# One V set copied into another tile, and two stores queued behind the wait for Wo

## The chip, the cores and the metric

The kernel runs on one core of one Trainium2 chip. The metric is the device time of one execution in microseconds (us), median of several runs.

## The reference

Two layers follow each other on 2048 rows of 512 numbers. The first is an attention over segments with a memory that is handed from segment to segment, the second a gated MLP with a mixing over rows:

```python
for s in range(n_seg):                      # 64 segments of 32 rows
    h = concat([mem, xs])                   # 8 memory rows + 32 rows
    q, k, v = h @ Wq, h @ Wk, h @ Wv        # 32 heads of 128
    p = softmax(where(mask, q @ k.T * scale, -1e9))
    o = (p @ v) @ Wo
    mem = o[:, :M]                          # next segment's memory
    outs.append(o[:, M:])
h  = x + concat(outs)                       # x was normalized for the attention
z  = gelu(layernorm(h) @ w_in); z1, z2 = halves(z); z2 = layernorm(z2)
h2 = h + (z1 * (w_sp @ z2 + b_sp)) @ w_out
```

Segments depend on each other through `mem`, so the kernel runs 64 steps one after the other.

## The kernel before

**Steps and groups.** One step is one segment (`for s in range(NSEG)`). A step multiplies 32 columns: 8 memory rows and the first 24 rows of its segment. The last 8 rows of each segment are taken out of the step, 16 segments at a time: a *batched group* `ck` (four of them) holds 16 × 8 = 128 rows, whose Q, K and V are computed with full tiles, in pieces that are put between the work of earlier steps. V of a group is made as eight *sets* `n` of 128 × 512 numbers by `vx_mm(ck, n, bank)`. `vx_evac(ck, n, bank, eng)` copies a set from PSUM into an SBUF tile (ScalarE at L488, VectorE at L490) and stores it to the DRAM buffer `vext_d` (L494). Step `s` gets its part back by `load_vx(s)` into `Vx` (L511).

**The tiles.** Sets of group 0 lie in `part` (eight rows of tiles, free at the start). Sets of all later groups share the two halves of `Vs`, by turns: `vcnt` counts them in program order. `partx` holds the *batched output rows* (the output of the rows that were taken out of the steps); it is first written in step 6 and stored at L773.

**The order on the queues.** The program is written as one list; each operation goes to its engine's queue in that order, and an emitter derives its waits from names of what it reads and writes ("tokens"): who writes a tile waits for all who still read it, stores included. Nearly all DMAs are issued by SyncE (SP in the profile), in program order, so a wait ahead of one DMA holds all those behind it. An argument `after` adds a wait; `behind()` names TensorE's last instruction in the program so far.

**The start.** The weights are loaded first: Wq, Wv, Wk, and then `Wo` in four quarters (L922). Of group 0, the first two segments' piece of each set is stored at once; the pieces for segments 2 to 5 of sets 2 to 7 are put aside in `vrest[0]` and issued later, the rest (`vrest[1]`) in steps 0 to 2. In step 0 the program then has, among others: the Q, K and V of segment 0 (`QK`, L539; `V_half`, L645), the batched Q/K/V left over, set 0 of group 1 (`start_v(0, 1)`, copied by VectorE), scores (L590) and softmax, set 1 of group 1 (copied by ScalarE), and behind it these four:

```python
vx_evac(1, 1, 5, "act")
for f in vrest[0]:
    f([em.last_w[("Wo", 3)]])     # after the last quarter of Wo
wT_read(0, 0)                     # L851: a transposed read of w_sp into wst
load_xe(3, 1)                     # L303: rows of group 3 into xn
```

then `load_x(2, 0)` (L295: rows 256 to 383 into `xn`), the products with V (L670, L676), `wT_write(0, 0)` (L856), set 2 of group 1 (VectorE), the output product with `Wo` (L708, in two halves, evacuated by ScalarE at L727), the memory for the next segment (L735, L738), the first Q and K products of step 1, set 0 of group 2 (ScalarE), and the copy of the mask into PSUM for step 1 (L574). Step 1 goes on with its Q and K products, which ScalarE evacuates (`QK_evac`, L550) and VectorE transposes (L558).

Of the kernel before, what the change touches and what calls it, by code (L numbers as in the profile page):

```python
# [169 lines left out]
def fast_path(nc, st, keep, flags, A_x, A_mem0, A_Wq, A_Wk, A_Wv, A_Wo, A_seg_len, B_w_in, B_w_sp, B_b_sp, B_w_out, out):  # L170
# [25 lines left out]
    em = Emitter(n_dma_sems=40)  # L196

    def sb(name, shape, dt):
        return st.enter_context(nc.sbuf_tensor("f_" + name, shape, dt))
# [32 lines left out]
    partx = sb("partx", [128, 512], BF)  # L232
# [38 lines left out]
    def PB(b):  # L271
        return ("ps", b)

    def sp(fn, **k):
        return em.add("sp", fn, dma=True, **k)
# [4 lines left out]
    def act(fn, **k):  # L280
        return em.add("act", fn, **k)

    def dve(fn, **k):
        return em.add("dve", fn, **k)
# [13 lines left out]
    def xbuf(j):  # L298
        return (xn[:, j, :], [("xn", j)]) if j < 2 else (part[:, j, :], [("part", j, 0), ("part", j, 1)])

    def load_xe(ck, j, queue="sp"):
        t, tok = xbuf(j)
        em.add(queue, lambda e: e.dma_start(t, xe[CK * ck:CK * ck + CK, XM:SEG, :]), dma=True, writes=tok)  # L303
# [176 lines left out]
    def vx_evac(ck, n, bank, eng="act", queue="sp"):  # L480
        if ck == 0:
            t, tok = part[:, n, :], [("part", n, 0), ("part", n, 1)]
        else:
            j = vcnt[0] % 2
            vcnt[0] += 1
            t, tok = Vs[:, j, :], [("Vs", j)]
        if eng == "act":
            act(lambda e: e.activation(out=t, in_=ps[:, bank, :], func=ACT.Copy, scale=VSC), reads=[PB(bank)], writes=tok)  # L488
        else:
            dve(lambda e: e.tensor_scalar(out=t, in0=ps[:, bank, :], scalar1=VSC, scalar2=None, op0=ALU.mult), reads=[PB(bank)], writes=tok)  # L490
        def store(i0, i1, ks, queue="sp", after=()):
            r = slice(8 * i0, 8 * i1)
            dst = vext_d[ck, n, r, :, :].rearrange("p r e -> p (r e)")
            em.add(queue, lambda e: e.dma_start(dst, t[r, :]), dma=True, reads=tok, writes=[("vext", ck, n, k) for k in ks], after=after)  # L494

        if ck:
            store(0, CK, (0,), queue)
        else:
            store(0, 2, (0,), queue)
            if n < 2:  # L500
                store(2, CK, (1, 2))
            else:
                vrest[0].append(lambda after=(): store(2, 6, (1,), after=after))
                vrest[1].append(lambda: store(6, CK, (2,)))

    vcnt, vrest = [0], ([], [])
# [247 lines left out]
    def behind():  # L754
        return [em.by_eng["pe"][-1]]
# [19 lines left out]
    def px_load(rb):  # L775
        i0 = 4 * rb % 8
        for g in range(4):
            sp(lambda e, g=g: e.dma_start(part[32 * g:32 * g + M, i0:i0 + 4, :], px_d[rb, g].rearrange("j r d -> r j d")),
               reads=[("pxd", rb)] + [("part", i0 + j, k) for j in range(4) for k in range(2)], writes=[("pm", rb % 2, g)])
# [69 lines left out]
    def wT_read(i, k):  # L849
        r = slice(8 * k, 8 * k + 8)  # L850
        sp(lambda e: e.dma_start_transpose(out=wst[:, r, :], in_=B_w_sp[i * 64:(i + 1) * 64, 1024 * k:1024 * k + 1024]),  # L851
           writes=[("wst", k)], after=behind())
# [39 lines left out]
    def start_v(n, ck=0):  # L892
        start_group(vx_mm, vx_evac, ck, n)
# [27 lines left out]
    for hq in range(4):  # L921
        sp(lambda e, hq=hq: e.dma_start(w_o[:, 8 * hq:8 * hq + 8, :], wor[:, 8 * hq:8 * hq + 8, :]), writes=[("Wo", hq)])  # L922
        em.mark_const(("Wo", hq))


    class Gap:
# [23 lines left out]
    def vx_group(ck, n):  # L950
        gx.append([lambda dc=dc: vx_mm(ck, n, XB, dc) for dc in range(DC)] + [lambda: vx_evac(ck, n, XB, "dve")])

    def vx_atoms(ck, n):
        mms = [lambda ck=ck, n=n, dc=dc: vx_mm(ck, n, VXB, dc) for dc in range(DC)]
        gv.add(VXB, mms, lambda eng: vx_evac(ck, n, VXB, eng))
# [59 lines left out]
    for s in range(NSEG):  # L1015
# [3 lines left out]
            w2_load()  # L1019
        if j4 == 3 and rb > 0:  # L1020
            px_load(rb - 1)
        if s > 0:
            wT_read(s // 2, s % 2)

        def qk_piece(pi):
            QK(s, QKP[pi], range(2 if pi < 2 else 1 if pi == 2 and s else 0, DC))
# [67 lines left out]
        sm_rcp(1)  # L1094
        if s == 0:
            vx_evac(1, 1, 5, "act")
            for f in vrest[0]:
                f([em.last_w[("Wo", 3)]])
            wT_read(0, 0)
            load_xe(3, 1)  # L1100
        if s > 0:
            v_second()
        if j4 == 1:
# [965 lines left out]
def build_kernel(nc, A_x, A_mem0, A_Wq, A_Wk, A_Wv, A_Wo, A_seg_len, B_x, B_w_in, B_w_sp, B_b_sp, B_w_out, out):  # L2069
    args = (A_x, A_mem0, A_Wq, A_Wk, A_Wv, A_Wo, A_seg_len, B_w_in, B_w_sp, B_b_sp, B_w_out, out)  # L2070
    flags = {}
    with contextlib.ExitStack() as keep:
        with contextlib.ExitStack() as st:
            em, sems, dsems = fast_path(nc, st, keep, flags, *args)
# [83 lines left out]
```

## Time and profile before

| | |
|---|---|
| median of 3 runs | 838.24 us (837.37 to 839.92) |
| profiled execution | 840.62 us |
| its span, first to last instruction | 838.9 us |
| mean granted TensorE clock | 0.997 |
| TensorE busy | 824.4 us (98%) |
| VectorE / ScalarE / GpSimd busy | 475.9 / 514.2 / 145.0 us |
| DMA | 80.54 MB, mean 96 GB/s |

The profile shows one execution. PE is TensorE, PEld its weight load, DVE VectorE, ACT ScalarE, POOL GpSimd, and SP or SPq SyncE, which issues DMAs. A row of a timeline has the start in us from the span's start, the duration, engine, line, operation, output and input tile, shapes and count; in brackets stands the idle time of the engine ahead of it and who ended it. A row of the chain has start, duration and what the end of the program was waiting for at that time. A row of the windows has the stretch, its length, the busy time of each engine with its number of instructions, the granted TensorE clock (1.00 is full), the busy share of the DMA engines and GB/s. A row of the waits has the engine and line that waited, for whom, the sum in us, how many times, and the longest.

### The profile page before, as it was taken

Reading aid. Unit: us, or ns where it says so; the run is one execution under the profiler, and the core shown is the slowest. Engines: PE = TensorE matmul, PEld = TensorE weight load, DVE = VectorE, ACT = ScalarE, POOL = GpSimd, SP = SyncE. Lnnn points to the kernel's source line nnn. Section 1 sums busy time; section 2 is a strip of 40 time slices with the busy share of each in tenths; the row PEclk is TensorE's granted clock in tenths of the full one; section 3 lists DMA queues with packets and bytes.
Section 4 is the critical chain, followed back from the end, with each engine's and each line's share of the span. In section 5 each row is a group of like instructions: output and inputs, shape, how many; then the busy total and the mean of one; then the engine's idle time right before and its main releaser. Section 6 shows DMA issues by size and latency. Waiting matters only on the chain.

```text
span 838.9 us, 48365 instructions
## 1 busy us (share of the span) xinstructions
PE 824.4 (98%) x21963; PEld 484.4 (58%) x21963; DVE 475.9 (57%) x1221; ACT 514.2 (61%) x1549; POOL 145.0 (17%) x412
## 2 busy tenths in 40 slices
PE   7999999999999999999999999999999999999998
PEld 7755565656566555655566656555665554444443
DVE  3546565656566555666556556565655576653344
ACT  2467777777777777777777777676666676300000
POOL 5202111121121111112211121111111123200000
PEclk9999999999999999999999999999999999999999
DMA  9975222122222222222212122333343278223101
GB/s 313 386 214 108 69 60 68 49 68 60 61 63 58 65 60 65 63 73 58 67 50 72 48 70 72 103 85 85 78 83 84 73 253 260 90 101 103 42 13 48
DMA packets 107652, 80.54 MB, mean 96 GB/s; under 512 B 49672, under 2 KB 97040, under 8 KB 107440
## 3 DMA queue, kind: packets, MB, share of 16 engines
q1 hardware_dynamic: 105712, 74.82, 30.8%
q8 instruction: 174, 2.85, 1.5%
q10 hardware_dynamic: 1504, 2.36, 0.9%
q14 instruction: 38, 0.31, 0.1%
q0 software_dynamic: 224, 0.20, 0.1%
HBM read 43.72 MB, written 23.13 MB: 80 GB/s over the span
## 4 chain that ended last, share of the span: by engine, by line
PE 92%; SPq 5%; DMA 1%; issue 0%; ACT 0%; DVE 0%; POOL 0%; POOLq 0%
PE f_ps L539 27%; PE f_ps L708 14%; PE f_ps L645 13%; PE f_ps L1266 12%; PE f_ps L426 4%; PE f_ps L764 4%; SPq L313 3%; PE f_ps L1360 3%; PE f_ps L1259 3%; PE f_ps L670 3%; PE f_ps L476 2%; PE f_ps L830 2%; PE f_ps L590 1%; DMA f_arena<-in_A_Wo_dram 1%; SPq L922 1%; PE f_ps L1226 1%
## 5 line engine op out<-in xcount | busy, mean ns | idle before, releaser
L539 PE MATMUL f_ps<-f_arena,f_hT 128*32 128x512 bf16 (+1 forms) x5120 | 238.5, 337 | 0.4
L539 PEld LDWEIGHTS f_ps<-f_arena,f_hT 128*32 128x32 bf16 x5120 | 124.4, 96 | 89.0 <-ACT f_hT L738 20.0
L550 ACT ACTIVATE f_Tst<-f_ps 128x512 bf16<-128x512 f32 (+2 forms) x320 | 143.4, 510 | 36.1 <-PE f_ps L539 28.5
L645 PE MATMUL f_ps<-f_arena,f_hT 128*32 128x512 bf16 x2048 | 139.8, 379 | 0.0
L708 PE MATMUL f_ps<-f_arena,f_cT 128*32 128x256 bf16 x4096 | 130.1, 273 | 2.2 <-DMA f_arena<-in_A_Wo_dram 1.3
L635 POOL TENSOR_TENSOR f_E_sb<-f_R_sb,f_E_sb 128x64 bf16<-128x64 f32 x128 | 47.5, 371 | 411.0 <-ACT f_R_sb L627 411.0
L708 PEld LDWEIGHTS f_ps<-f_arena,f_cT 128*32 128x32 bf16 x4096 | 97.0, 96 | 27.5 <-ACT f_cT L694 17.3
L558 DVE STREAM_TRANSPOSE f_QT<-f_Tst 128x256 uint32<-128x256 uint32 x128 | 57.1, 446 | 93.2 <-ACT f_Tst L550 93.2
L657 DVE TENSOR_SCALAR f_V_sb<-f_ps 128x512 bf16<-128x512 f32 (+1 forms) x128 | 71.4, 558 | 52.4 <-PE f_ps L645 52.4
L1266 PE MATMUL f_ps<-f_arena 128*128 128x512 bf16 x448 | 100.5, 379 | 0.0
L1266 PEld LDWEIGHTS f_ps<-f_arena 128*128 128x128 bf16 x448 | 43.7, 98 | 52.9 <-issue 0.3
L694 ACT ACTIVATE f_cT<-f_ps 128x160 bf16<-128x160 f32 (+1 forms) x192 | 55.6, 329 | 26.0 <-PE f_ps L676 25.4
L696 DVE TENSOR_SCALAR f_cT<-f_ps 128x256 bf16<-128x256 f32 x128 | 48.4, 420 | 36.7 <-PE f_ps L676 36.7
L604 ACT ACTIVATE f_E_sb<-f_ps 128x224 bf16<-128x224 f32 x128 | 46.3, 362 | 36.6 <-PE f_ps L616 35.4
L727 ACT ACTIVATE f_part<-f_ps 128x256 bf16<-128x256 f32 x128 | 49.3, 385 | 20.6 <-PE f_ps L708 16.1
L558 DVE STREAM_TRANSPOSE f_KT<-f_Tst 128x256 uint32<-128x256 uint32 (+2 forms) x192 | 58.4, 330 | 4.5 <-ACT f_Tst L550 1.8
L645 PEld LDWEIGHTS f_ps<-f_arena,f_hT 128*32 128x32 bf16 x2048 | 47.1, 95 | 19.8 <-issue 0.4
L738 ACT ACTIVATE f_hT<-f_ps 128x16 bf16<-128x16 f32 x126 | 23.3, 185 | 45.8 <-PE f_ps L735 45.8
L1272 DVE TENSOR_TENSOR f_arena<-f_ps,f_arena 128x512 f32<-128x512 f32 x28 | 19.3, 690 | 52.5 <-PE f_ps L1266 50.5
L627 ACT ACTIVATE f_R_sb<-f_R_sb 128x160 f32<-128x160 f32 x128 | 43.3, 338 | 4.0
L576 DVE CAST f_ps<-f_mask 128x224 f32<-128x224 bf16 x80 | 29.9, 373 | 26.9 <-ACT f_hT L406 24.5
L426 PE MATMUL f_ps<-f_arena,f_hTe 128*32 128x512 bf16 x640 | 41.9, 379 | 0.0
(127 smaller groups left out, 1157.8 us busy)
## 6 DMA issues: line engine op xcount, KB each, us to landing
wT_d<-f_wst SPq DMA_DIRECT2D x64, 128.0 KB
f_arena<-wT_d SPq DMA_DIRECT2D x32, 256.0 KB
f_arena<-in_A_Wv_dram SPq DMA_DIRECT2D x4, 1024.0 KB
f_arena<-in_A_Wk_dram SPq DMA_DIRECT2D x4, 1024.0 KB
f_arena<-in_A_Wo_dram SPq DMA_DIRECT2D x4, 1024.0 KB
f_Vx<-vext_d SPq DMA_DIRECT2D x62, 64.0 KB
vext_d<-f_Vs SPq DMA_DIRECT2D x24, 128.0 KB
zp_d<-f_Vs SPq DMA_DIRECT2D x20, 112.0 KB
```

The source lines that it names most:

```text
L426: pe(lambda e, c=c, rhs=rhs: e.matmul(ps[32 * c:32 * c + 32, bank, :], lhsT=hTe[:, ck, dc, 32 * sg:32 * sg + 32], rhs=rhs, start=(dc == 0) ...
L539: pe(lambda e, dc=dc, c=c, rhs=rhs: e.matmul(ps[32 * c:32 * c + 32, bank, 0:32 * nh], lhsT=hT[:, sl, dc, :], rhs=rhs, start=(dc == 0), sto ...
L550: act(lambda e: e.activation(out=st_.rearrange("p (hp i r) -> p hp i r", i=32, r=2), in_=ps[:, bank, 0:64 * np_].rearrange("p (hp r i) -> ...
L558: dve(lambda e: e.transpose(out=dst, in_=src), reads=tok, writes=[(nm, b, k) for k in halves(b, p0, np_)])
L635: pool(lambda e: e.tensor_tensor(out=ev, in0=rv, in1=ev, op=ALU.mult), reads=[("R", b), ("Ex", b)], writes=[("Ex", b)])
L645: pe(lambda e, dc=dc, c=c, c0=c0: e.matmul(ps[32 * c:32 * c + 32, bank, 0:w], lhsT=hT[:, sl, dc, :], rhs=w_v[:, dc, c0:c0 + w], start=(dc ...
L657: dve(lambda e: e.tensor_scalar(out=dst, in0=src, scalar1=VSC, scalar2=None, op0=ALU.mult), reads=[PB(bank)], writes=tok)
L694: act(lambda e: e.activation(out=dst, in_=src, func=ACT.Copy, scale=UNSC), reads=[PB(bank)], writes=tok)
L696: dve(lambda e: e.tensor_scalar(out=dst, in0=src, scalar1=UNSC, scalar2=None, op0=ALU.mult), reads=[PB(bank)], writes=tok)
L708: pe(lambda e, h=h, g=g, i=i, b=b, c=c: e.matmul(ps[32 * g:32 * g + 32, bank, 0:d1 - d0], lhsT=cTh[:, i, 8:40], rhs=w_o[:, h, d0:d1], star ...
L727: act(lambda e: e.activation(out=part[:, s % 8, d0:d1], in_=ps[:, bank, 0:d1 - d0], func=ACT.Copy), reads=[PB(bank)], writes=[("part", s % ...
L1266: pe(lambda e: e.matmul(ps[:, bank, 0:TB], lhsT=z2[:, sc, fb * 128:(fb + 1) * 128], rhs=wTb[tb % 2][:, :, sc, :], start=first, stop=last), ...
```

## The change

Three things are edited. Set 0 of group 1 is copied into `partx` and stored from there, and does not count in the turns of `Vs`. The held pieces `vrest[0]`, with their wait for the last quarter of `Wo`, come right behind the loads of `Wo` in the program. The first transposed read `wT_read(0, 0)` and `load_xe(3, 1)` come at the top of step 0. On SyncE's queue the stores of sets 0 and 1 of group 1 now stand behind all of these.

```diff
     def vx_evac(ck, n, bank, eng="act", queue="sp"):
         if ck == 0:
             t, tok = part[:, n, :], [("part", n, 0), ("part", n, 1)]
+        elif (ck, n) == (1, 0):
+            t, tok = partx[:], ["partx"]
         else:
             j = vcnt[0] % 2
             vcnt[0] += 1
...
         em.mark_const(("Wo", hq))
+    for f in vrest[0]:
+        f([em.last_w[("Wo", 3)]])
...
-        if s > 0:
-            wT_read(s // 2, s % 2)
+        wT_read(s // 2, s % 2)
+        if s == 0:
+            load_xe(3, 1)
...
         if s == 0:
             vx_evac(1, 1, 5, "act")
-            for f in vrest[0]:
-                f([em.last_w[("Wo", 3)]])
-            wT_read(0, 0)
-            load_xe(3, 1)
```

## The prediction

> **What bounds the kernel now.** I read the page's first part, then its chain, then the chain in order of time around the four `Wo` loads, because that is the place in the program that the change touches.
>
> ```profile
> span 838.9 us, 48365 instructions
> PE 824.4 (98%) x21963; PEld 484.4 (58%) x21963; DVE 475.9 (57%) x1221; ACT 514.2 (61%) x1549; POOL 145.0 (17%) x412
> PE 92%; SPq 5%; DMA 1%; issue 0%; ACT 0%; DVE 0%; POOL 0%; POOLq 0%
> ...
> 42.84 12.13 DMA f_arena<-in_A_Wo_dram
> 54.97 0.04 issue
> 55.01 1.38 PE f_ps L708 x44
> ...
> 57.40 3.05 PE f_ps L539 x72
> 60.45 0.10 PE f_ps L590 x15
> ```
>
> TensorE is busy 98% of the span and holds 92% of the chain. So there is no slack later on in which a delay could be taken back: a microsecond in which TensorE stands still in the first steps is a microsecond at the end. The chain passes from DMA to TensorE at 54.97, when the last quarter of `Wo` lands; from 55.01 it is TensorE's, and 60.45 is the first score product of step 1.
>
> Next the place itself: SyncE's queue, and TensorE's wait.
>
> ```profile
> 50.15 2.17 SPq L494 DMA_DIRECT2D vext_d<-f_Vs  x2
> 54.99 3.31 SPq L494 DMA_DIRECT2D vext_d<-f_part  x6
> 58.34 1.33 SPq L851 DMA_TRANSPOSE f_wst<-in_B_w_sp_dram  x1
> 59.71 0.57 SPq L303 DMA_DIRECT2D f_xn<-in_A_x_dram  x1
> 60.33 0.58 SPq L295 DMA_DIRECT2D f_xn<-in_A_x_dram  x1
> 61.34 0.34 SPq L856 DMA_DIRECT2D wT_d<-f_wst  x1
> ...
> 53.17 0.55 PE L708 MATMUL f_ps<-f_arena,f_cT 128*32 128x256 bf16 x12
> 55.01 1.38 PE L708 MATMUL f_ps<-f_arena,f_cT 128*32 128x256 bf16 x44 [1.29 <-DMA f_arena<-in_A_Wo_dram]
> 57.25 3.20 PE L539 MATMUL f_ps<-f_arena,f_hT 128*32 128x512 bf16 x72
> 60.28 0.27 PE L590 MATMUL f_ps<-f_QT,f_KT 128*32 128x40 bf16 x16
> ```
>
> The two stores of 128 KB (sets 0 and 1 of group 1) are issued from 50.15. The six held rests of group 0 go out at 54.99, at once when `Wo` has landed; behind them SyncE issues without a break the transposed read (58.34), the row load L303 (59.71) and the row load L295 (60.33). TensorE's output product L708 starts with 12 matmuls, which need the first three quarters of `Wo`, and stands still 1.29 us for the fourth. That 1.29 us is all that an earlier landing of `Wo` can give.
>
> **The change part by part.** *The two large stores leave the time before 54.97.* Do they delay `Wo` now? VectorE tells, since its third copy (set 2 of group 1) writes the buffer that the first store reads:
>
> ```profile
> 55.36 0.69 DVE L490 TENSOR_SCALAR f_Vs<-f_ps 128x512 bf16<-128x512 f32 x1 [1.59 <-DMA vext_d<-f_Vs]
> 59.67 0.45 DVE L558 STREAM_TRANSPOSE f_KT<-f_Tst 128x256 uint32<-128x256 uint32 x1
> 48.00:52.00 4.00, 3.72 (x97) 1.99 (x95) 1.45 (x4) 2.95 (x8) 0.81 (x2) 1.00 1.03 330
> 52.00:55.00 3.00, 1.72 (x64) 0.90 (x64) 0.89 (x3) 1.08 (x5) 0.64 (x2) 1.00 0.40 138
> ```
>
> The store issued at 50.15 releases VectorE at 55.36, 5.2 us later and just after the last of `Wo` (54.97): what was issued later on SyncE's queue came out later, so the stores stood behind `Wo`, not before it. From 52 to 55 the engines are busy only 0.40, so `Wo`'s tail is not short of bandwidth either. Ends for the gain: 0, and 0.8 us if the 262 KB had to go through first at the 330 GB/s of the row before. I take 0, since the order of landing is the nearer evidence. [...]
>
> VectorE's 1.59 us wait goes too (set 2 now has a buffer that nobody reads yet). It gives nothing: VectorE's next work, the transposes of step 1, ends what TensorE waits for at 59.67 + 0.45 = 60.12.
>
> *The buffers change places.* Set 0 goes to the row tile, so the alternation of the two-deep `Vs` starts one set later. Before: set 0 in half 0, set 1 in half 1, set 2 in half 0, and set 0 of group 2 in half 1. After: set 1 in half 0, set 2 in half 1, and set 0 of group 2 in half 0. That last copy is ScalarE's, at the end of step 0, and now overwrites what the store of set 1 reads. It must wait until that store has landed.
>
> ```profile
> 57.49 0.18 ACT L738 ACTIVATE f_hT<-f_ps 128x16 bf16<-128x16 f32 x1 [0.37 <-PE f_ps L735]
> 57.57 0.59 ACT L488 ACTIVATE f_Vs<-f_ps 128x512 bf16<-128x512 f32 x1
> 58.05 0.37 ACT L574 ACTIVATE f_ps<-f_mask 128x224 f32<-128x224 bf16 x1
> 58.55 2.32 ACT L550 ACTIVATE f_Tst<-f_ps 128x512 bf16<-128x512 f32 x5
> ```
>
> The copy (L488) runs at 57.57 and no wait stands before it: the store of set 1 went out around 52. After the change that store stands on SyncE's queue behind the wait for `Wo` (54.99), the six rests, the transposed read and L303. Nothing of these is faster than before, so it reaches the place where L295 stands now: set 0's store at 60.33, set 1's about 0.38 us later (the 0.34 us of the equal store L856 and a gap), at 60.7. When does it land? Nearest is the same form of transfer, the 128 KB store of the row tile, with the load that waits for it:
>
> ```profile
> 115.79 0.32 SPq L773 DMA_DIRECT2D px_d<-f_partx  x1
> 118.88 1.31 SPq L778 DMA_DIRECT2D f_part<-px_d  x4
> ...
> SPq L778 <- DMA px_d<-f_partx: 23.1, 12, 2.8
> ```
>
> Twelve such waits take 23.1 us, 1.9 us each behind the issue, and this one row bounds issue to landing by 3.1 us. So 60.7 + 0.34 + 1.9 = 63.0 us. Lower end: the queue gave things out in order, and the transposed read of 58.34 had landed only when L856 was issued at 61.34; so not before 61.3. Upper end: 5.2 us as behind `Wo`, 65.9. ScalarE's copy therefore moves from 57.57 to 63.0, by 5.4 us (ends 3.7 and 8.3).
>
> Behind it on ScalarE, in program order, stand the mask copy (L574) and the five evacuations of step 1's Q and K products (L550). TensorE can still run the 72 matmuls L539 to 60.45, since their banks are free; then the score product (60.28 now) waits for transposes that wait for L550. Its slack is 60.28 − 60.12 = 0.16 us. So TensorE stops for 5.4 − 0.16, **5.2 us** (ends 3.5 and 8.1), from 60.45 to about 65.6. Nothing hides this: VectorE and GpSimd have no other work for step 1, and TensorE takes its matmuls in program order.
>
> *The clock.* The same trace shows what a standstill of this length did near the start:
>
> ```profile
> 10.65 1.57 PE L449 MATMUL f_ps<-f_hTe,f_arena 128*128 128x128 bf16 x16 [3.31 <-DMA f_arena<-in_A_Wq_dram]
> 8.00:11.00 3.00, 0.35 (x7) 0.38 (x8) 0.00 (x0) 0.00 (x0) 2.03 (x12) 1.00 1.05 378
> 11.00:14.00 3.00, 3.00 (x32) 3.00 (x30) 0.89 (x2) 0.60 (x1) 2.16 (x10) 0.50 1.05 400
> 14.00:17.00 3.00, 3.00 (x53) 3.00 (x51) 0.89 (x2) 1.62 (x4) 2.23 (x9) 0.93 1.07 364
> ```
>
> After 3.31 us of idleness the granted clock was 0.50 from 11 to 14, and 0.93 on the mean of the next 3 us, so 3 + 3 × 0.07 / 0.5 = 3.4 us at half speed. Work bound by TensorE loses half of that, 1.7 us. Ends 0 and 1.7; I take **1.0**, as ScalarE paces part of the score stage (its 2.32 us of L550 come first) and the slow stretch may begin inside the idle time. By the row alone the clock falls, as the new standstill is longer than 3.31 us. [...]
>
> *What else is moved, at nothing.* The rests of group 0, the transposed read and L303 keep their time: they were released by `Wo` before and are now; the transposed read's new condition, the first Q product of step 0, is long past. GpSimd's two early loads of `Vx` read other pieces and wait for none of this. L295 is passed by two stores and goes out 0.8 us later (61.1); its reader is VectorE's normalization in step 1, itself 5 us later. L856 and the next stores move by under 1 us behind TensorE work that moves by five. The row tile's first other use is step 6. Without that cover each would cost at most the 0.8 us of two issues.
>
> *Sum.* Against the profiled execution: 840.62 us (its span 838.9 and 1.7 outside) + 5.2 + 1.0 = 846.8. That execution lies 2.4 us above the median of the runs shown, so on the median 838.24 + 6.2 = **844.4 us**.
>
> **The rivals.** *Clock stays up*: the standstill without the slow stretch, 838.24 + 5.2 = 843.4. [...] Against it: the 0.50 after the shorter wait.
>
> *Not slower: the stores did delay `Wo`, and nothing new waits.* This needs the store of set 1 to land before ScalarE comes to the copy, that is `Wo` to land some 5 us earlier, or the copy to find another buffer. The gain would then be 0.8 us, at most the 1.29 us of TensorE's wait: 837.0 to 837.4. For it: the wait at 55.01 is real and on the chain. Against it: the order of landing, and 1.29 us is far from 5.
>
> *It does nothing*: ScalarE's copy does not meet the store, 838.2. It would need the sets to be copied in another order than the rows show (49.4, 51.4, 55.36, 57.57 by start).
>
> ```profile
> 49.43 0.69 DVE L490 TENSOR_SCALAR f_Vs<-f_ps 128x512 bf16<-128x512 f32 x1 [1.33 <-PE f_ps L476]
> 51.37 0.58 ACT L488 ACTIVATE f_Vs<-f_ps 128x512 bf16<-128x512 f32 x1
> ```
>
> **How the numbers follow.** Standstill with the slow stretch, 844.4: 0.55. Standstill alone, 843.4: 0.37. Gain without a new wait: 0.05. Nothing: 0.01. A gain from something that no row shows: 0.02. A measurement of this kernel can tell about 0.3%, 2.5 us, from no change; the small gain and the nothing lie within that, so faster 0.02, same 0.06, slower 0.92. The range goes from the shortest standstill without slow clock, 838.24 + 3.5 = 841.7, taken as 841.8, to the longest with the whole slow stretch, 838.24 + 8.1 + 1.7 = 848.0.
>
> **What would show it.** Right: ScalarE's L488 near 63 with about 5 us of idleness before it, put down to the store from `Vs`; L574, L550 and the score product shifted alike; a hole in TensorE from about 60.5 to 65.6; a second stretch at 0.50 after it; L708's 1.29 us wait for `Wo` unchanged; later steps as long as before. Wrong: L488 at its old place; or `Wo` landing well before 54.97; or the hole filled by later steps becoming shorter.

## The result, and the profile after

The changed kernel takes 844.65 us (median of 6 runs, 843.25 to 848.13) against 837.75 us (6 runs) of the kernel before: a ratio of 1.0084, with a 95% interval of 1.0062 to 1.0105. It is slower by 6.9 us. The profiled execution of the changed kernel took 844.35 us, close to its median; that of the kernel before (840.62) lay 2.9 us above its own, so the two spans differ by only 3.7 us, and the loss has to be read at its place, not from the spans.

The page's first lines and the chain in order of time (start, duration, what the end was waiting for), after:

```profile
span 842.6 us, 48367 instructions
PE 825.7 (98%) x21963; PEld 486.3 (58%) x21963; DVE 475.8 (56%) x1221; ACT 513.6 (61%) x1549; POOL 145.0 (17%) x412
```

```profile
40.52 12.29 DMA f_arena<-in_A_Wo_dram
52.81 0.04 issue
52.86 1.39 PE f_ps L710 x44
...
55.25 2.21 PE f_ps L541 x40
57.45 0.18 SPq L853
57.63 0.05 issue
57.68 0.57 SPq L303
58.25 0.05 issue
58.30 0.58 SPq L496
58.88 0.04 issue
58.92 2.12 DMA vext_d<-f_Vs
61.05 0.02 issue
61.07 0.60 ACT f_Vs L490
61.67 0.25 ACT f_ps L576
61.92 1.01 ACT f_Tst L552 x2
```

The lines of the kernel that are named here stand two lower in the file than before (L708 is now L710), save L303 and L295. Where the chain of before stayed with TensorE from 55.01 on, it now leaves it for SyncE's queue (the transposed read, the row load L303, the store of set 0), then for the store of set 1 until 61.05, ScalarE's copy, the mask, and the first two evacuations. `Wo` landed at 52.81 here and at 54.97 in the trace of before. Most of that difference is older than anything that the change touches: the first Q and K products of step 0 already start at 32.19 here and at 34.69 before. So times are counted from `Wo`'s landing.

ScalarE's timeline, then TensorE's, after:

```profile
61.07 0.60 ACT L490 ACTIVATE f_Vs<-f_ps 128x512 bf16<-128x512 f32 x1 [5.55 <-DMA vext_d<-f_Vs]
61.57 0.35 ACT L576 ACTIVATE f_ps<-f_mask 128x224 f32<-128x224 bf16 x1
61.85 2.31 ACT L552 ACTIVATE f_Tst<-f_ps 128x512 bf16<-128x512 f32 x5
```

```profile
52.86 1.39 PE L710 MATMUL f_ps<-f_arena,f_cT 128*32 128x256 bf16 x44 [1.34 <-DMA f_arena<-in_A_Wo_dram]
55.09 3.20 PE L541 MATMUL f_ps<-f_arena,f_hT 128*32 128x512 bf16 x72
63.45 0.32 PE L592 MATMUL f_ps<-f_QT,f_KT 128*32 128x40 bf16 x16 [5.16 <-DVE f_KT L560]
72.75 3.20 PE L541 MATMUL f_ps<-f_arena,f_hT 128*32 128x512 bf16 x72
```

ScalarE's copy waited 5.55 us for the store from `Vs`; before, it had no wait at all. TensorE stood still for 5.16 us. Its wait for `Wo` is 1.34 us, as before (1.29).

A measure that needs no equal start: from TensorE's restart after `Wo` (L708, now L710) to the Q and K products of step 2. Before it is 67.42 − 55.01 = 12.41 us, now 72.75 − 52.86 = 19.89 us, a shift of **7.48 us**. In the three kernels below that lose nothing, the same stretch takes 12.08, 12.40 and 12.45 us, so the measure is good to some 0.3 us. From TensorE's restart to the end of the span the changed kernel takes 842.6 − 52.86 − (838.9 − 55.01) = 5.9 us longer, so most of the shift is kept to the end. Before:

```profile
67.42 3.20 PE L539 MATMUL f_ps<-f_arena,f_hT 128*32 128x512 bf16 x72
```

The 2.32 us beyond the standstill (7.48 − 5.16) can be seen in the windows (stretch, length, busy time of PE, PEld, DVE, ACT, POOL with counts, granted clock, DMA share, GB/s), after:

```profile
58.40:61.80 3.40, 0.00 (x0) 0.00 (x0) 0.00 (x0) 0.73 (x2) 0.00 (x0) 1.00 0.75 228
61.90:65.20 3.30, 1.75 (x36) 0.83 (x40) 1.96 (x6) 2.42 (x7) 0.00 (x0) 0.50 0.46 130
65.30:68.60 3.30, 3.30 (x68) 1.68 (x64) 1.42 (x4) 1.80 (x6) 0.65 (x2) 0.50 0.10 27
68.70:72.00 3.30, 3.30 (x132) 2.19 (x128) 2.28 (x7) 1.49 (x7) 0.64 (x2) 1.00 0.30 84
```

The clock was 0.50 for two stretches, from 61.8 to 68.6, and TensorE worked in them for 1.75 + 3.30 us.

### The profile page after: what moved, and what is told of

Same layout as the page of the kernel before. It is cut to its first block, busy times and chain, and to the rows that moved or that the text cites. A ratio compares the mean times of both kernels' runs of the same rounds, so it can differ in the third digit from the quotient of the medians.

```text
span 842.6 us, 48367 instructions
## 1 busy us (share of the span) xinstructions
PE 825.7 (98%) x21963; PEld 486.3 (58%) x21963; DVE 475.8 (56%) x1221; ACT 513.6 (61%) x1549; POOL 145.0 (17%) x412
## 4 chain that ended last, share of the span: by engine, by line
PE 93%; DMA 3%; SPq 2%; DVE 1%; issue 0%; ACT 0%; POOL 0%
PE f_ps L541 26%; PE f_ps L710 14%; PE f_ps L647 13%; PE f_ps L1267 11%; PE f_ps L426 4%; PE f_ps L766 4%; PE f_ps L1361 3%; PE f_ps L672 3%; PE f_ps L476 3%; PE f_ps L1260 2%; PE f_ps L832 2%; PE f_ps L449 2%; PE f_ps L592 1%; DMA f_arena<-in_A_Wo_dram 1%; SPq L924 1%; PE f_ps L613 1%
## 5 line engine op out<-in xcount | busy, mean ns | idle before, releaser
L541 PEld LDWEIGHTS f_ps<-f_arena,f_hT 128*32 128x32 bf16 x5120 | 126.1, 96 | 87.4 <-ACT f_hT L740 20.0
L710 PE MATMUL f_ps<-f_arena,f_cT 128*32 128x256 bf16 x4096 | 129.5, 273 | 1.7 <-DMA f_arena<-in_A_Wo_dram 1.3
L710 PEld LDWEIGHTS f_ps<-f_arena,f_cT 128*32 128x32 bf16 x4096 | 96.2, 96 | 26.6 <-ACT f_cT L696 18.0
L647 PEld LDWEIGHTS f_ps<-f_arena,f_hT 128*32 128x32 bf16 x2048 | 47.9, 96 | 19.8 <-issue 0.8
```

The source lines that it names most:

```text
L541: pe(lambda e, dc=dc, c=c, rhs=rhs: e.matmul(ps[32 * c:32 * c + 32, bank, 0:32 * nh], lhsT=hT[:, sl, dc, :], rhs=rhs, start=(dc == 0), sto ...
L647: pe(lambda e, dc=dc, c=c, c0=c0: e.matmul(ps[32 * c:32 * c + 32, bank, 0:w], lhsT=hT[:, sl, dc, :], rhs=w_v[:, dc, c0:c0 + w], start=(dc ...
L710: pe(lambda e, h=h, g=g, i=i, b=b, c=c: e.matmul(ps[32 * g:32 * g + 32, bank, 0:d1 - d0], lhsT=cTh[:, i, 8:40], rhs=w_o[:, h, d0:d1], star ...
```

## The experiments

The theory: ScalarE's copy of set 0 of group 2 waits for the store of set 1, which the change has queued behind `Wo`, the six pieces and two reads; TensorE loses that wait, and some more while its clock is low. The rivals: holding costs by itself, through SyncE; the other tile or the shifted turns cost; holding gains at `Wo` and something else loses. The kernels ran on several chips, whose medians of the kernel before differ (835.5, 836.7 and 840.4 us), so ratios are compared, and the shifts by the measure above. Line numbers differ by up to four between these kernels.

**A free buffer for the copy.** Both stores stay held.

```diff
         elif (ck, n) == (1, 0):
             t, tok = partx[:], ["partx"]
+        elif (ck, n) == (1, 1):
+            t, tok = xo[:, 1, :], [("xo", 1)]
```

> The changed kernel, with set 1 of group 1 copied into a tile that is free then (a row of xo), so that ScalarE's copy of set 0 of group 2 finds a buffer that no store still reads; both large stores stay held behind the wait for Wo. My theory (the whole loss comes from that copy waiting for the held store of set 1): no idle time ahead of it, no hole in TensorE, no slow stretch, 837.8 us, within 0.3% of before. Rival 1 (holding costs by itself: SyncE is late with the loads and stores behind the two stores): 844 to 845. Rival 2 (holding lets Wo land earlier, which the copy's wait has covered up): TensorE's wait for Wo falls from 1.3 us to 0.5 or less, 837.0.

Measured: 835.49 against 835.53 us, ratio 1.0000 (0.9991 to 1.0008). ScalarE's timeline and TensorE's:

```profile
55.08 0.59 ACT L492 ACTIVATE f_Vs<-f_ps 128x512 bf16<-128x512 f32 x1
```

```profile
52.52 1.39 PE L712 MATMUL f_ps<-f_arena,f_cT 128*32 128x256 bf16 x44 [0.94 <-DMA f_arena<-in_A_Wo_dram]
64.97 3.20 PE L543 MATMUL f_ps<-f_arena,f_hT 128*32 128x512 bf16 x72
```

No wait, a shift of 64.97 − 52.52 − 12.41 = 0.04 us. One more buffer takes away the whole loss, so holding by itself costs nothing that can be told, and it gains nothing either.

**The tile alone, nothing held.**

```diff
+        elif (ck, n) == (1, 0):
+            t, tok = partx[:], ["partx"]
```

> The kernel before with one part of the change: set 0 of group 1 goes to the row tile, so the turns of Vs shift by one; nothing is held, and the queue's order is the old one. My theory: ScalarE's copy of set 0 of group 2 now follows the store of set 1, but that store goes out before Wo has landed and lands just after it (VectorE was released at 55.4 by the store ahead of it), some 2 us before the copy comes (57.6): no wait, 837.8 us; VectorE's 1.6 us wait before set 2 is gone and brings nothing. Rival (the other tile or the shifted turns cost by themselves): 844 to 845.

Measured: 835.86 us, ratio 1.0005 (0.9995 to 1.0015); the copy has no wait, and TensorE's wait for `Wo` was 1.24 us. The tile and the turns cost nothing.

**Both stores held, the old buffers.** The two lines above taken out of the changed kernel.

> The changed kernel without the row tile: both large stores are held, and the sets take turns in the two halves of Vs as before. My theory: set 0 of group 2 then overwrites set 1's half as well, whose store is just as late, so the hole in TensorE is the same 5 to 5.5 us with the slow stretch behind it, 844.6 us (843.5 to 846); VectorE's copy of set 2 waits too, for the store of set 0, some 7 us, off the path. Rival (the shifted turns are what makes ScalarE wait): 837.8.

Measured: 842.27 us, ratio 1.0084 (1.0068 to 1.0099). VectorE's row, ScalarE's and TensorE's:

```profile
59.66 0.69 DVE L490 TENSOR_SCALAR f_Vs<-f_ps 128x512 bf16<-128x512 f32 x1 [8.24 <-DMA vext_d<-f_Vs]
```

```profile
60.14 0.60 ACT L488 ACTIVATE f_Vs<-f_ps 128x512 bf16<-128x512 f32 x1 [5.10 <-DMA vext_d<-f_Vs]
```

```profile
62.52 0.32 PE L590 MATMUL f_ps<-f_QT,f_KT 128*32 128x40 bf16 x16 [4.70 <-DVE f_KT L558]
```

The loss is the same. What the row tile takes away, VectorE's wait of 8.24 us, is off the path; the wait that counts is not touched by it.

**One store held.** Two edits of the kernel before. In both, set 0 goes to the row tile, one store goes out at once as before, the other behind `load_xe(3, 1)`:

```diff
-        if ck:
+        if (ck, n) == (1, 1):          # the other kernel: (1, 0)
+            vheld.append(lambda: store(0, CK, (0,), queue))
+        elif ck:
             store(0, CK, (0,), queue)
...
             load_xe(3, 1)
+            for f in vheld:
+                f()
```

> The changed kernel's buffers (set 0 in the row tile, turns of Vs shifted), but only the store of set 1 is held: the store of set 0 goes out at once, before Wo has landed. My theory (ScalarE waits for the store of set 1 alone): the hole stays, shorter by the one issue of 0.6 us that has gone ahead of it, 4.6 us, with a slow stretch where the clock falls: ratio 1.0055 to 1.008. Rival (both stores must be held to cost, or set 0's is the one that counts): 1.000.

> The counterpart: the same buffers, the store of set 1 goes out at once, and only the store of set 0, from the row tile, is held until the loads behind Wo have been issued. My theory: nobody waits for the row tile until step 6, so no wait ahead of ScalarE's copy, no hole, ratio 1.000. Rival (a large store behind the wait for Wo costs whoever reads its tile, through SyncE or the DMA engines): 1.004 or more.

Measured: set 1 held 842.59 against 836.66 us, ratio 1.0070 (1.0057 to 1.0083), ScalarE's wait 5.46 us; set 0 held 837.39, ratio 1.0006 (0.9995 to 1.0017), no wait. ScalarE's timeline in the one and in the other:

```profile
61.93 0.60 ACT L490 ACTIVATE f_Vs<-f_ps 128x512 bf16<-128x512 f32 x1 [5.46 <-DMA vext_d<-f_Vs]
```

```profile
55.37 0.59 ACT L490 ACTIVATE f_Vs<-f_ps 128x512 bf16<-128x512 f32 x1
```

The store of set 1 alone makes the loss. The expected 0.6 us less did not show: in that execution the six pieces took 3.90 us on SyncE, against 3.44.

**The held stores earlier.** The transposed read and L303 are issued behind the two stores:

```diff
-        wT_read(s // 2, s % 2)
-        if s == 0:
-            load_xe(3, 1)
+        if s > 0:
+            wT_read(s // 2, s % 2)
...
             vx_evac(1, 1, 5, "act")
+            wT_read(0, 0)
+            load_xe(3, 1)
```

> The changed kernel with the transposed read and the load of group 3's rows issued behind the two held stores, not ahead of them; the six held pieces stay ahead. In the profile of the changed kernel these two issues took 1.32 + 0.57 us and two gaps of 0.05, 2.0 us. [...] Rival (what counts is being behind the wait for Wo at all): 1.008.

Measured: 840.95 us, ratio 1.0047 (1.0029 to 1.0065). SyncE's queue and TensorE:

```profile
56.21 0.42 SPq L496 DMA_DIRECT2D vext_d<-f_partx  x1
56.68 0.43 SPq L496 DMA_DIRECT2D vext_d<-f_Vs  x1
```

```profile
52.81 1.38 PE L710 MATMUL f_ps<-f_arena,f_cT 128*32 128x256 bf16 x44 [1.06 <-DMA f_arena<-in_A_Wo_dram]
60.88 0.28 PE L592 MATMUL f_ps<-f_QT,f_KT 128*32 128x40 bf16 x16 [2.63 <-DVE f_KT L560]
67.78 3.20 PE L541 MATMUL f_ps<-f_arena,f_hT 128*32 128x512 bf16 x72
```

The store went out 56.68 − 52.81 = 3.9 us after `Wo`, against 58.92 − 52.81 = 6.1 in the changed kernel: 2.2 us sooner, and the standstill is 2.5 us shorter. The shift is 67.78 − 52.81 − 12.41 = 2.56 us, all of it standstill; the clock stayed at 1.00. In these two profiles the standstill follows the lateness of that one store, about a microsecond for a microsecond. By the medians the loss is 4.3 us, more than this one profile shows and than the ratio of 1.003 to 1.004 that was expected of a hole of 3.2 us with the clock at full; the interval holds both.

**TensorE kept busy in the hole.** Dummy matmuls, whose result nobody uses, ahead of the score product of step 1 in the changed kernel; 72 narrow ones, 44 narrow ones, 18 wide ones:

```diff
+            for _ in range(72 if s == 1 else 0):      # then 44
+                pe(lambda e: e.matmul(ps[:, 4, 0:160], lhsT=onesrc[:, 0:128], rhs=onesrc[:, :], start=True, stop=True),
+                   reads=["onesrc"], writes=[PB(4)])
```

> The changed kernel with 72 matmuls of 128x160 on constants (their result is used by nobody) in TensorE's queue ahead of the score product of step 1, where TensorE stands still: some 4.8 us of work within the hole. It takes the slow clock away and leaves the wait. In the profile of the changed kernel the hole was 5.2 us, and TensorE lost another 2.1 us in the stretch at 0.50 after it. My theory: ScalarE's wait of 5.5 us stays, the granted clock stays at 1.00, 842.5 us. Rival (the slow stretch costs nothing, since ScalarE sets the pace there): 844.6. Rival (the dummy work itself delays the score product): over 845.

Measured: 842.65 against 835.53 us, ratio 1.0087 (1.0072 to 1.0102). The clock stayed at 1.00, but the dummies (5.15 us from 60.07) kept the score product back to 65.15, while its transposes had ended at 64.03. In this execution TensorE came to its output product (54.30) only after `Wo` had landed (the pieces behind it went out from 53.03), so ScalarE's wait was shorter too, 4.34 us. The profiled execution does not account for this ratio: from step 1's to step 2's Q and K products it took 71.97 − 56.93 = 15.04 us, against 67.42 − 57.25 = 10.17, a shift of 4.9 us, and it was the fastest of its five runs (841.36).

> The changed kernel with 44 dummy matmuls of 128x160 ahead of the score product of step 1. Of the 72 in the run before, each took 71.5 ns, 5.15 us in all, and they kept the score product back 1.1 us beyond its transposes; 44 take 3.1 us and end well before them. ScalarE's wait stays, TensorE's standing still is cut to 1 to 2 us. My theory (the loss is the 5.2 us wait, plus about 2 us where the clock falls behind it): clock at 1.00 after the hole, and a loss of 5.2 us, ratio 1.006. Rival (the slow stretch has no price of its own at the end, later steps give it back): 1.008, as with the changed kernel.

Measured: 846.38 against 836.66 us, ratio 1.0120 (1.0103 to 1.0137): worse than the changed kernel, and foretold neither by the theory (1.006) nor by the rival (1.008).

> The changed kernel with 18 matmuls of 128x512 on constants (result used by nobody) ahead of the score product of step 1: about 3.9 us of work in the hole, with 36 instructions where the 44 narrow ones were 88 with their weight loads and pulled a fetch of instructions into the time in which the held store should land. My theory: no fetch between 57 and 63 us, ScalarE's wait about 5.4 us again and not 7, the clock stays at 1.00 through step 1, and the next step starts 5.2 us late, not 7.5: ratio 1.0062 (1.005 to 1.0075). Rival (the long wait of that run came from TensorE's work in the hole as such): a wait of 7 us again, 1.010 or more.

Measured: 846.21 against 840.44 us, ratio 1.0075 (1.0046 to 1.0104), which holds both the theory's 1.0062 and the rival's 1.010. ScalarE's wait was 7 us in both of the last two, as the rival had it, and the fetch of instructions that the theory did without was there again. ScalarE's timeline with the 44, and with the 18:

```profile
62.42 0.60 ACT L490 ACTIVATE f_Vs<-f_ps 128x512 bf16<-128x512 f32 x1 [6.98 <-DMA vext_d<-f_Vs]
```

```profile
62.15 0.60 ACT L490 ACTIVATE f_Vs<-f_ps 128x512 bf16<-128x512 f32 x1 [7.01 <-DMA vext_d<-f_Vs]
```

The store of set 1 was issued at 58.60 and 58.27 there, so it took 3.8 and 3.9 us to release ScalarE; it took 2.15 in the changed kernel (58.92 to 61.07) and 1.8 to 2.2 in every other kernel of this study in which ScalarE waits for it. The DMA queues in the time from that issue to the release, with the 44, and in the changed kernel (packets, MB, share):

```profile
q1 hardware_dynamic: 757, 0.69, 57.0%
q8 instruction: 1, 0.02, 2.6%
```

```profile
q1 hardware_dynamic: 568, 0.53, 79.5%
```

A fetch of instructions ran while the store was on its way, with the 44 and likewise with the 18 (one packet of 0.02 MB), and in none of the other kernels where ScalarE waits for the store, save that with the 72 one began at 61.22, half a microsecond ahead of the release. In the changed kernel no fetch began between 54.23 and 65.68; that TensorE's standstill put it off is inferred.

The marks of landing in the traces say what the fetch goes with. Each of these stores left 16 of them, one for each part that landed. With the 44, 15 of them had landed by 60.61 and the last at 62.40; with the 18, by 60.38 and at 62.13. In the kernel with the free buffer, which has no dummy matmuls and no hole, a fetch began at 59.32 and the store of set 1 shows the same: 15 parts by 60.29, the last at 62.24, where nobody waited for it. In the changed kernel, without a fetch, all 16 landed between 60.77 and 61.05; with the 72, where TensorE worked all through but the fetch began only at 61.22, between 61.26 and 61.68. So the late part goes with the fetch and not, as the rival had it, with TensorE's work as such. No run moves the fetch alone, so that it holds up the one part stays inferred.

In the execution with the 18, the clock stayed at 1.00: dummies 3.83 us, standstill 2.62 and 0.16, in sum 6.61, and the shift was 71.43 − 52.48 − 12.41 = 6.54 us. So without a slow stretch nothing is lost beyond the hole itself.

**The changed kernel once more**, on the chip of the last runs.

> The changed kernel itself once more, on the chip of the three runs below, so that its loss can be set beside theirs. From the runs so far, with the steps counted from the end of step 0: a hole of about 5.2 us, and a stretch at 0.50 that costs TensorE 0.41 to 0.45 of the time that it works in it, 1.1 to 2.3 us. Ratio 1.0075 to 1.009.

Measured: 847.38 against 840.44 us, ratio 1.0072 (1.0047 to 1.0097). Standstill 5.22 us; the shift was 71.37 − 52.45 − 12.41 = 6.51 us. The slow stretch lasted half as long as in the first profile:

```profile
59.40:62.80 3.40, 0.00 (x0) 0.00 (x0) 0.64 (x2) 2.00 (x5) 0.00 (x0) 1.00 0.74 240
62.80:66.20 3.40, 3.10 (x72) 1.50 (x76) 2.01 (x6) 1.97 (x7) 0.00 (x0) 0.50 0.31 82
66.30:69.70 3.40, 3.40 (x124) 1.95 (x120) 2.12 (x7) 2.17 (x9) 1.39 (x4) 1.00 0.22 63
```

**Two tries at a version that beats both**, on the kernel before. The first holds the stores that are queued ahead of `Wo`: sets 0 and 1 of group 0 are copied into `partx` and `xo[:, 1]`; the first two segments' piece still goes out at once, and the other pieces go with `vrest`.

> The kernel before with the opposite idea: nothing of group 1 is held; sets 0 and 1 of group 0 are copied into tiles that are free until steps 6 and 8 (the row tile and a row of xo), and their two stores of 112 KB, now issued ahead of the loads of Wo, are held until Wo has landed. My theory (what is queued ahead of Wo delays it, what is queued behind does not): Wo lands 0.6 us earlier (229 KB at 390 GB/s), TensorE's wait for it falls from 1.3 to about 0.7 us, and no copy waits: ratio 0.9993, at the edge of what can be told. Rival (Wo's tail has nothing to do with those bytes): wait unchanged, 1.000.

Measured: 840.22 against 840.44 us, ratio 0.9993 (0.9971 to 1.0015), not told from no change. TensorE's wait for `Wo` was 0.45 us, but the same trap opened one step later:

```profile
66.37 0.60 ACT L488 ACTIVATE f_Vs<-f_ps 128x512 bf16<-128x512 f32 x1 [1.38 <-DMA vext_d<-f_Vs]
```

```profile
69.72 0.28 PE L587 MATMUL f_ps<-f_QT,f_KT 128*32 128x40 bf16 x16 [1.95 <-DVE f_KT L555]
```

With two more stores on SyncE's queue, the next store from `Vs` was late for ScalarE's next copy, and TensorE stood still 1.95 us in step 2. The second try changes only TensorE's order in step 0:

```diff
+            early, late_ = [(0, 0), (0, 1), (2, 0), (1, 0), (1, 1), (3, 0)], [(2, 1), (3, 1)]
+            Wo_cb(early, OB, 0, OC)              # pairs (c, b); 4 matmuls each
+            Wo_cb(early, OB2, OC, D, [x3])
+            Wo_cb(late_, OB, 0, OC)
+            part_evac(s, OB, 0, OC)
+            Wo_cb(late_, OB2, OC, D)
```

> The kernel before with TensorE's output product of step 0 in another order: both halves first take all heads whose quarter of Wo lands early (24 matmuls each), and the last quarter's 8 and 8 come last. Before, 12 matmuls ran ahead of the wait. My theory (the 1.3 us wait for the last quarter is on the path and only needs work to cover it): 36 more matmuls at 31 ns are 1.1 us, the wait falls to about 0.2 us and the kernel gains 1.0 us, ratio 0.9988. Rival (the mixed order costs as much as it covers, since the copies of the products with V are not ready earlier): 1.000.

Measured: 839.96 against 840.44 us, ratio 0.9986 (0.9965 to 1.0007). In its profile no wait of TensorE for `Wo` is left, and one of 0.46 us stands before the last 6 matmuls; the interval holds 1, so whether it beats the kernel before stays open.

## Why the prediction was right, point by point

The forecast was 844.4 us and 6.2 us lost; measured were 844.65 and 6.9. That the time came within 0.3 us is partly luck: the three runs of before that the forecast started from had a median 0.5 us above that of all six, which made up for most of the 0.7 us that the loss was too small.

- **The buffers change places, and ScalarE's copy waits.** Right. It was foretold for 63.0 where `Wo` landed at 54.97, 8.0 us behind it; it came at 61.07 − 52.81 = 8.3. The store of set 1 was issued 6.1 us behind `Wo`, not 5.7, since the six pieces took 3.44 us (3.31 before) and set 0's store 0.58 us, not 0.34; issue to release was 2.15 us against 2.24.
- **TensorE stops for 5.2 us.** Right: 5.16 and 5.22. Each part of the argument was tried by itself: the store of set 1 (yes), set 0's (no), the tile (no), a free buffer (no loss), an earlier issue (a shorter loss).
- **The clock.** That it would fall behind the standstill was right, and the size was off. The term was 1.0 us with ends 0 and 1.7; measured by shift less standstill it is 2.32 us in one profile of the changed kernel and 1.29 in the other, and 1.16 and 1.47 in the kernels that hold both stores with the old buffers, and set 1's alone. So the term was too small in all four, and its upper end too low for the first. What was off there is the length: 3.4 us were taken from the event at 11 us, and in the first profile the clock was at 0.50 for 6.8 us. I had also let ScalarE's pace shorten it too much: TensorE loses 2.32 of the 5.2 us that it works at 0.50 (63.45 to 68.6), about 0.45 of it. Where the clock stayed high (the 18 wide matmuls), nothing was lost beyond the hole.
- **What was weighed.** That the stores might delay `Wo`: with both held and a free buffer, the ratio is 1.0000 (0.9991 to 1.0008), so the 0.8 us which that reading would have given (0.9990) lies just outside; a smaller gain isn't excluded. Whether the clock falls: it fell in both profiles of the changed kernel, and where both stores or set 1's alone were held, with standstills of 4.70 to 5.22 us (in the last two the 16 V products behind the standstill took 1.90 us, against 1.03 in the free-buffer kernel's next step), and stayed up at 2.63 us. In all four the 3.3 us ahead of the fall show no work of TensorE (as the two rows with 0.00 above; 58.6 to 61.9 and 61.0 to 64.3 in the other two). With the 44 matmuls it is different. The standstill was 3.43 us, up to 64.80, and the clock fell between 66.0 and 66.2, when TensorE had been at work again for 1.2 us or more, behind a stretch of 3.40 us in which it had worked 1.20 us:

```profile
64.80 0.28 PE L592 MATMUL f_ps<-f_QT,f_KT 128*32 128x40 bf16 x16 [3.43 <-DVE f_KT L560]
```

```profile
59.20:62.60 3.40, 2.17 (x32) 1.97 (x29) 0.00 (x0) 0.18 (x1) 0.00 (x0) 1.00 0.61 196
62.60:66.00 3.40, 1.20 (x56) 0.66 (x59) 1.96 (x6) 3.07 (x8) 0.00 (x0) 1.00 0.35 106
66.20:69.40 3.20, 3.20 (x48) 1.42 (x40) 1.60 (x4) 1.91 (x6) 1.01 (x3) 0.50 0.15 38
```

  So here the clock fell without TensorE being idle right up to the fall. The reading from the row, by the length of the standstill, fits all these profiles: the clock fell behind 3.31, 3.43 and 4.70 to 5.22 us and stayed up behind 1.95 (the first try above), 2.62 and 2.63. Where the border lies is open, as each kernel but the changed one has a single profiled execution: in the first try TensorE worked 1.35 us of 3.30 (66.50 to 69.80), and the clock stayed at 1.00.
- **Moved at nothing.** Right as a whole: the free-buffer kernel moves the same reads, loads and stores and has ratio 1.0000.
- **The rivals.** "Gain at `Wo`" and "does nothing" are excluded for the changed kernel by its interval. "Clock stays up" (5.2 us lost, a ratio of 1.0062) lies at the interval's lower end, so the time alone hardly tells it from the forecast; the two profiles, with 0.50 behind the standstill in each, do. That the clock stays up behind a standstill of this length, which had a chance of 0.37, is shown by no run: it fell to 0.50 in all four profiles with 4.70 to 5.22 us. TensorE's wait for `Wo` was 1.34 and 0.80 us in the two profiles of the changed kernel, 0.40 to 1.06 in the others that hold both stores and have such a wait, and 1.29 and 1.24 where nothing was held. That leaves room for a gain of some tenths of a microsecond, which the ratios can't tell.

## What to carry to other kernels

When a store is put behind a wait, look for who writes its buffer next, count through the ring's turns with the new order, and compare the time of that copy with the store's landing, not with its issue. A ring of two whose stores may be held needs as many buffers as there are copies before the wait ends; here one more tile made the same hold free. And that something stands in the same queue as a transfer is no reason for the transfer's lateness until the order of landing says so.

## What the runs showed of the hardware

- After 3.31 us of standstill (near the start of the kernel before), after 3.43 us (the 44 dummy matmuls) and after 4.70 to 5.22 us (four profiles) the granted clock went to 0.50 each time; after 2.62 and 2.63 us it stayed at 1.00. It was at 0.50 for 3.4 us in the kernel before and in the second profile of the changed kernel (62.8 to 66.2), and for 6.8 us in the first (61.8 to 68.6). In the longer case TensorE worked 1.75 of the first 3.30 us at 0.50, and the clock stayed down; in the second profile it worked 3.10 of 3.40, and the clock came back. In the four profiles the work in these stretches lost 1.2 to 2.3 us.
- A store of 128 KB needed 1.8 to 2.2 us from issue to release of the waiting engine, and 3.8 to 3.9 us in the two executions in which one packet of instructions was fetched between the two. In these two, 15 of the store's 16 parts had landed 2.0 to 2.1 us after the issue, and the last 1.8 us later.
